# A searched instruction order with longer latencies, one block's K and V loads on the GpSimd queue, and early memsets on VectorE

## The chip, the cores and the metric

The kernel runs on one core of a Trainium2 chip. A core has five engines with instruction streams of their own: TensorE (PE, matrix products), VectorE (DVE), ScalarE (ACT), GpSimd (POOL) and SyncE (SP, which here only issues transfers). The metric is the device time of one execution in microseconds (us); the median of several executions is compared.

## The reference

An attention in which every query sees only six chunks of 32 keys, followed by a two-layer network with an ELU. Cut to what matters:

```python
# q, k, v: (4 batches, 8 heads, 768 positions, 64); w_in (512, 2048); w_out (2048, 512)
k_min, k_max = min and max of k over each chunk of 32 keys          # 24 chunks
ub = sum_d(maximum(q * k_min, q * k_max))                            # upper bound per query and chunk
ub = where(causal by chunk, ub, -1e9)
top_chunks = the 6 chunks with the largest ub, per query
scores = q @ k.T / sqrt(64);  masked to the chosen chunks and to keys not after the query
attn = exp(scores - max) / sum
x = attn @ v, heads side by side                                     # 3072 tokens x 512
h = x @ w_in
g = where(h > 0, h, exp(min(h, 0)) - 1)                              # ELU
out = g @ w_out
```

## The kernel before

The kernel cuts the 3072 tokens into nine blocks: three of 256 queries for the first batch, two of 384 for each of the others. Heads are worked on in four pairs. Each block goes through the same stages, and each stage is a set of small operations that are recorded first, each with an engine, an assumed duration, an assumed latency and what it reads and writes:

```python
def prep_k(j, i):   # pair j, block i: K turned on PE, chunk minima and maxima on DVE, copy to lhs
    turn_in(psk, k_ld, w // P)                                        # PE transposes (float32), L480
    op("DVE", ..., lambda: reduce(kmx..., AOT.max), ...)              # L500
    op("DVE", ..., lambda: reduce(ksts[bp][:, 0, j, cs], AOT.min), ...)
    # copy to lhs: ACT directly for blocks 0 and 1 (L507), else ACT (L512) and a transfer (L515)
def prep_q(j, i):   # Q turned on PE, QTf on ACT (L530), rhs on ACT (L534) or POOL (L538), relu on DVE (L541)
def select(i):      # bounds of all chunks (PE, L559), then on DVE: transposes (L570), MAX8 (L577),
                    # compare (L581), and the mask written into rhs: by DVE transposes (L587) for
                    # blocks 0 to 2, by a transpose and eight transfers (L593, L597) for later ones
def attend(j, i, at):  # scores (PE, L621), exp (ACT, L637), causal triangle (DVE, L648),
                       # weighing of V (PE into o_bank, L670), division (DVE, L679, L681),
                       # turned to xt by PE (L689) or by a transposing transfer (L694)
def mlp(i, at):     # per 128 hidden units: 4 matmuls (L709), exp (ACT, L713), minus 1 (POOL, L715),
                    # min and max into gT (DVE, L717); then 16 matmuls per 128 tokens with w_out (L728)
```

A scheduler inside the kernel then places all operations in time with these assumed durations, taking on each engine the ready operation with the smallest priority number. `SHIFTS` adds a number to the priority for each stage, engine and block; the table was found by search over that model. The resulting order, not the times, becomes the program:

```python
            if done is not None:
                done.end = clock + 750                # a transfer is seen 750 ns after its last byte
...
            else:
                o.end = t + o.occ + o.lat
...
    for o in plan.ops:
        o.prio = o.prio0 + (SHIFTS[o.key[0][0], o.eng][o.key[0][1]] if o.key[0] else 0.0)
    plan.run()
    pe = 0.0
    with tc.manual_schedule():
        for o in plan.order:
            if o.eng == "PE":
                if o.start < FILL_END:
                    for _ in range(int((o.start - pe - 100) / FILL_NS) if pe else int((o.start - FILL_FROM) / 95)):
                        nc.tensor.matmul(o_bank[:, 400:512], lhsT=junk, rhs=junk[:, 0:112], start=True, stop=True)
                pe = o.start + o.occ
            o.fn()
```

The matmuls on `junk` (L836) are fillers: they compute nothing that is used and keep TensorE busy where the model sees a gap in the first 70 us.

At the start, constants and padding are written, mostly by GpSimd, and the first loads are issued from three queues. `SW_LOADS` names those of the GpSimd queue, `SW_ORDER` their order, `ACT_LOADS` those of which one half goes to ScalarE's queue. A gate, a copy of one element of the first K tile, keeps the GpSimd queue from starting before that tile is there:

```python
SW_LOADS = ("v0", "q1", "v1", "k2", "q2", "v2")
ACT_LOADS = ("k0", "q0", "k1")
SW_ORDER = ("v0", "q1", "v1", "wi0", "wi1", "wi2", "wi3", "k2", "q2", "v2", "wo0", "wo1", "wo2", "wo3")
...
    pool_op(150, lambda: nc.gpsimd.memset(junk, 0.0), [r_junk])
    for x in range(2):
        pool_op(650, lambda x=x: nc.gpsimd.memset(ksts[x], 0.0), ...)
    for s in range(NPAIR):
        init_vext(s)
    for h in range(2):
        for x in range(2):
            pool_op(360, lambda h=h, x=x: nc.gpsimd.memset(selb[x][h], 0.0), [r_selb[x][h]])
        pool_op(650, lambda h=h: nc.gpsimd.memset(rhs[0][64:96, h, :, 0:QSEL], 0.0), r_m[0][h])
    ...
        gate_ops.append(op("POOL", 120, 60, lambda: nc.gpsimd.tensor_copy(out=spot[:, 0:1], in_=gx.get()[0:1, 0, 0, 0:1]), ...))
```

Of the kernel before, what the change touches and what calls it, by code (L numbers as in the profile page):

```python
# [32 lines left out]
NPAIR = H // 2  # L33
# [17 lines left out]
PSM_PREP = (0, )  # L51
PSM_S = (0, )
MASK_DVE = (0,1,2)
SW_LOADS = ("v0", "q1", "v1", "k2", "q2", "v2")
ACT_LOADS = ("k0", "q0", "k1")
SW_ORDER = ("v0", "q1", "v1", "wi0", "wi1", "wi2", "wi3", "k2", "q2", "v2", "wo0", "wo1", "wo2", "wo3")
QC_ACT = (0, 1)
VC_ACT = ()
SW_GATE = ("k", 0)
# [4 lines left out]
CAPS = dict(psT=1, psS=2, psO=1, psM=4, kld=2, qld=2, vld=1, QTf=6, Qrl=6, kb=3, kmx=3, ubT=2, thr=2,  # L64
            msk=2, pt=9, rcp=2, on=3, xt=12, gT=6, e=4, osb=2)
RING = 64
FILL_NS = 500
FILL_FROM = 1500
FILL_END = 70e3
SHIFTS = {  # L70
    ('cast', 'POOL'): (20.57252, 6.8612, 30.20405, 34.41781, 25.32335, 14.40461, 26.6349, 11.90162, 25.68724),
    ('gate', 'POOL'): (13.59135, 0.0, 0.0, 0.0, 0.0, 0.0, 0.0, 0.0, 0.0),
    ('init', 'POOL'): (0.0, 2.28733, 0.0, 0.0, 0.0, 0.0, 0.0, 0.0, 0.0),
    ('init', 'SP'): (0.0, 0.0, -9.16794, 0.0, 0.0, 0.0, 0.0, 0.0, 0.0),
    ('kld', 'ACT'): (8.44149, -3.35541, 0.0, 0.0, 0.0, 0.0, 0.0, 0.0, 0.0),
    ('kld', 'SP'): (2.64524, 1.41433, 0.0, 19.17193, 19.24991, 15.09263, 15.30211, 16.29283, 21.31107),
    ('kld', 'POOL'): (0.0, 0.0, 0.38774, 0.0, 0.0, 0.0, 0.0, 0.0, 0.0),
    ('mlp_in', 'ACT'): (-0.05814, -2.04884, 12.26157, -1.88135, -2.65088, -4.49011, 9.3327, 8.76113, -19.73093),
    ('mlp_in', 'DVE'): (-1.73242, 3.97867, -1.47336, 9.41966, -10.49042, -8.87396, -12.71275, -12.8411, -15.53763),
    ('mlp_in', 'PE'): (4.09513, -2.56825, 21.51914, 0.57236, -12.4212, 2.60542, -2.43752, -8.17452, 3.48831),  # L80
    ('mlp_in', 'POOL'): (-2.43649, 11.70673, 2.23367, -14.23721, -5.69178, 14.90153, -11.32679, 8.9361, -11.19179),
    ('mlp_out', 'ACT'): (-12.88274, 0.81443, 16.77095, 16.67571, -11.88345, 9.70583, 0.95732, -8.4172, -1.17404),
    ('mlp_out', 'PE'): (13.70296, 13.79101, 25.0585, 31.67234, 12.47262, 15.64879, 21.01371, 0.27209, 18.2925),
    ('mlp_out', 'SP'): (-3.30971, -11.51233, -15.89764, -18.24659, -18.60542, -17.81261, -26.35693, -42.75655, -13.10907),
    ('prep_k', 'ACT'): (25.42091, 28.44317, 23.77021, 23.42552, 13.97171, 21.34953, 15.42692, 18.62561, 8.78796),
    ('prep_k', 'DVE'): (-0.54594, 19.16199, -1.31495, -4.02643, 4.07559, 21.34444, 2.30963, 13.60589, 3.98678),
    ('prep_k', 'PE'): (-11.58195, 3.17776, 12.63442, -8.97337, 3.48395, 2.91992, -14.39538, 4.89175, 2.89372),
    ('prep_k', 'SP'): (0.0, 0.0, -5.13913, -2.5227, -2.19514, 2.12301, -17.34079, 2.83345, -3.2583),
    ('prep_q', 'ACT'): (-5.44132, 13.02836, -8.90449, 17.58325, 14.42173, 12.5627, 34.41294, 25.56545, -14.46432),
    ('prep_q', 'DVE'): (34.05268, 22.68609, 13.28254, 24.29798, 22.86233, 18.30023, 26.52607, 17.39426, -1.03575),  # L90
    ('prep_q', 'PE'): (1.55827, 3.21992, -10.06088, -5.14194, -2.06832, 11.30076, 4.84068, 13.28142, -17.29924),
    ('prep_q', 'POOL'): (0.0, 0.0, 5.34856, 19.77789, 11.98652, -3.89053, 10.37057, 11.76628, -23.71212),
    ('qld', 'ACT'): (3.03879, 0.0, 0.0, 0.0, 0.0, 0.0, 0.0, 0.0, 0.0),
    ('qld', 'SP'): (-1.86639, 0.0, 0.0, 4.4756, 10.84559, 7.56364, -2.78613, 8.55013, 3.96718),
    ('qld', 'POOL'): (0.0, -13.20166, -16.00657, 0.0, 0.0, 0.0, 0.0, 0.0, 0.0),
    ('score', 'ACT'): (10.38182, 13.98097, 9.11548, 19.0005, 2.98314, 27.9414, -1.05566, 1.31311, 14.18917),
    ('score', 'DVE'): (-19.79772, 4.15071, 2.99001, -22.45535, -14.99666, -19.5343, -10.56439, -19.58759, -3.51749),
    ('score', 'PE'): (-4.26638, 7.52896, -6.42214, -0.75335, 6.37057, 12.51955, 6.09242, -2.75776, -4.26028),
    ('select', 'DVE'): (0.47921, -15.73633, 7.03029, -0.12414, -12.38193, 6.31401, -10.30796, 14.19953, -5.33831),
    ('select', 'PE'): (-24.6966, -18.87682, -19.68284, -16.23997, -30.84817, 2.75471, -0.87585, -4.04933, -12.62166),  # L100
    ('select', 'SP'): (0.0, 0.0, 0.0, -13.44596, -16.7602, -5.46409, -14.4042, 14.89348, -7.20168),
    ('vld', 'POOL'): (8.78219, 3.38089, -2.61859, 0.0, 0.0, 0.0, 0.0, 0.0, 0.0),
    ('vld', 'SP'): (0.0, 0.0, 0.0, 33.2739, 30.57728, 28.35083, 33.49035, 19.69352, 14.95572),
    ('w_in', 'POOL'): (-4.9889, 0.0, 0.0, 0.0, 0.0, 0.0, 0.0, 0.0, 0.0),
    ('w_out', 'POOL'): (-8.71011, 0.0, 0.0, 0.0, 0.0, 0.0, 0.0, 0.0, 0.0),
    ('weigh', 'DVE'): (11.1506, -8.59523, 21.73165, 3.04344, -9.17916, -0.955, 14.23334, -3.50298, 13.22401),
    ('weigh', 'PE'): (-14.42242, 4.04006, -5.56916, -12.49286, -15.03128, -12.17144, 11.16201, -20.81204, -2.27982),
    ('weigh', 'SP'): (0.0, -24.05575, -20.27905, -10.4246, -14.45262, -3.75467, -21.17209, -15.72941, 0.0),
}


# [38 lines left out]
class Plan:  # L150
# [37 lines left out]
    def run(self):  # L188
# [41 lines left out]
        while True:  # L230
# [35 lines left out]
                    dirty.add(e)  # L266
                    room = True
            if done is not None:
                done.end = clock + 750
                lanes[done.eng][done.lane] = done.end  # L270
                dirty.update(("SP", "ACT", "POOL"))
                leave(done, done.end)
                enter(done, done.end, True)
                continue
# [15 lines left out]
            if isinstance(o.lat, tuple):  # L290
                rings[o.eng].append([t + o.occ + o.lat[2], o.lat[0], o.lat[1], o])
                if o.eng != "POOL" and over(o.eng) > 1e-6:
                    full_rings[o.eng], free[o.eng] = free[o.eng], 1e18
                e = lane_of[o.eng]
                o.lane = turn[e]
                lanes[e][o.lane], turn[e] = 1e18, (o.lane + 1) % 8
                dirty.update(("SP", "ACT", "POOL"))
            else:
                o.end = t + o.occ + o.lat
                leave(o, o.end)  # L300
                enter(o, o.end, True)
        assert len(self.order) == len(self.ops)
# [4 lines left out]
def kernel(  # L307
# [120 lines left out]
    def load(dst, x, i, cls, at):  # L428
# [5 lines left out]
        for n in range(nt):  # L434
            at(n / nt)
            e = "POOL" if cls[0] + str(i) in SW_LOADS else "ACT" if cls[0] + str(i) in ACT_LOADS and n == 1 else "SP"

            def go(n=n, q=dict(SP=nc.sync, ACT=nc.scalar, POOL=nc.gpsimd)[e]):
                q.dma_start(out=xb.get()[:, n, :, :], in_=x[b, :, lo + P * n:lo + P * (n + 1)].rearrange("h p d -> p h d"))  # L439

            o = op(e, 890 if e == "POOL" else 600, (770, 159, 1000) if e == "POOL" else dma(64, 256), go,
                   writes=[r], hold=[xb], seq=[*(chain if e == "SP" else ()), *newest.get(cls, ())])
            newest[cls] = [o]
            if e == "SP":
                chain[:] = [o]
            if e == "POOL":
                sw.setdefault(cls[0] + str(i), []).append(o)
        for j in range(NPAIR):
            dst[j, i] = (xb, (r, ), slice(2 * j, 2 * j + 2))

# [303 lines left out]
    def casts(i):  # L754
        at = span(i - 1, 0.5 + SP_F[0], 0.5 + SP_F[1])
        plan.tag = ("cast", i)
        for j in range(NPAIR):
            at(j / NPAIR)
            cast_v(j, i)

    for s in range(NPAIR):
        init_lhs(s, "DVE")
    pool_op(150, lambda: nc.gpsimd.memset(junk, 0.0), [r_junk])
    for x in range(2):
        pool_op(650, lambda x=x: nc.gpsimd.memset(ksts[x], 0.0), [r for j in range(NPAIR) for r in r_kst[x][j]])
    for s in range(NPAIR):
        init_vext(s)
    for h in range(2):
        for x in range(2):
            pool_op(360, lambda h=h, x=x: nc.gpsimd.memset(selb[x][h], 0.0), [r_selb[x][h]])  # L770
        pool_op(650, lambda h=h: nc.gpsimd.memset(rhs[0][64:96, h, :, 0:QSEL], 0.0), r_m[0][h])
    pool_op(300, lambda: nc.gpsimd.tensor_copy(out=ident_b, in_=ident_f), [r_ident_b], [r_ident_f])
    pool_op(900, make_tri, [r_tri])
    gate_ops = []
# [13 lines left out]
    front(0)  # L788
    casts(0)
    plan.tag = ("init", 1)  # L790
    span(-0.5, 0.0, 0.1)
    for s in range(NPAIR, NSET):
        init_vext(s)
    load_kq(1)
# [36 lines left out]
    with tc.manual_schedule():  # L831
        for o in plan.order:
            if o.eng == "PE":
                if o.start < FILL_END:
                    for _ in range(int((o.start - pe - 100) / FILL_NS) if pe else int((o.start - FILL_FROM) / 95)):
                        nc.tensor.matmul(o_bank[:, 400:512], lhsT=junk, rhs=junk[:, 0:112], start=True, stop=True)  # L836
                pe = o.start + o.occ
            o.fn()
# [29 lines left out]
```

## Time and profile before

| | before |
|---|---|
| device time, median of 3 | 306.47 us (304.36 to 306.54) |
| span of the profiled execution | 302.4 us |
| busy PE / DVE / ACT / POOL | 279.0 / 204.9 / 201.3 / 138.9 us |
| mean granted TensorE clock | 0.96 of full |
| bytes moved by DMA | 36.23 MB, mean 120 GB/s |

How to read it: busy time is the time in which an engine has an instruction in flight. Matmuls overlap each other, so the busy time of PE is not the time that its work needs; that is read from how far apart the starts of matmuls lie when nothing holds them. The granted clock is the share of full speed at which TensorE was allowed to run. "Us to landing" of a transfer counts from its issue to the signal that the data is there.

### The profile page before, as it was taken

Reading aid. Unit: us, or ns where it says so; the run is one execution under the profiler, and the core shown is the slowest. Engines: PE = TensorE matmul, PEld = TensorE weight load, DVE = VectorE, ACT = ScalarE, POOL = GpSimd, SP = SyncE. Lnnn points to the kernel's source line nnn. Section 1 sums busy time; section 2 is a strip of 40 time slices with the busy share of each in tenths; the row PEclk is TensorE's granted clock in tenths of the full one; section 3 lists DMA queues with packets and bytes.
Section 4 is the critical chain, followed back from the end, with each engine's and each line's share of the span. In section 5 each row is a group of like instructions: output and inputs, shape, how many; then the busy total and the mean of one; then the engine's idle time right before and its main releaser. Section 6 shows DMA issues by size and latency. Waiting matters only on the chain.

```text
span 302.4 us, 7251 instructions
## 1 busy us (share of the span) xinstructions
PE 279.0 (92%) x2521; PEld 177.4 (59%) x2521; DVE 204.9 (68%) x658; ACT 201.3 (67%) x458; POOL 138.9 (46%) x285
## 2 busy tenths in 40 slices
PE   7466878999999899999999989999999999999994
PEld 7235645677857645666665546666556666554541
DVE  4567488799666979768579955874866646680420
ACT  1764767579829725997797259886398896671521
POOL 8796674024817624571069322581535100570420
PEclk9955797999999999999999999999999999999999
DMA  8769996149292565658239853924111012100101
GB/s 194 204 130 196 292 220 115 41 125 244 48 222 74 133 149 135 162 153 204 81 80 219 191 166 84 233 57 128 47 44 43 3 48 63 30 21 37 67 37 70
DMA packets 88805, 36.23 MB, mean 120 GB/s; under 512 B 76224, under 2 KB 84928, under 8 KB 88768
## 3 DMA queue, kind: packets, MB, share of 16 engines
q1 hardware_dynamic: 80464, 27.64, 36.3%
q0 software_dynamic: 5184, 7.34, 12.0%
q10 hardware_dynamic: 3120, 0.79, 1.2%
q8 instruction: 20, 0.33, 0.4%
q14 instruction: 17, 0.14, 0.1%
HBM read 27.26 MB, written 6.29 MB: 111 GB/s over the span
## 4 chain that ended last, share of the span: by engine, by line
PE 64%; DVE 14%; DMA 7%; POOL 6%; SPq 3%; ACT 2%; issue 2%; POOLq 0%; DVEq 0%; ACTq 0%
PE psM L728 22%; PE psM L709 18%; PE psS L621 10%; PE o_bank L670 6%; PE psT L480 5%; DVE gT L717 3%; DMA rhs<-msk 3%; DVE rhs L587 2%; POOL e L715 2%; SPq L439 2%; DMA vld<-in_v_dram 2%; DVE kmx L500 2%; PE psT L559 1%; DMA qld<-in_q_dram 1%; DVE pt L648 1%
## 5 line engine op out<-in xcount | busy, mean ns | idle before, releaser
L715 POOL TENSOR_SCALAR e<-e 128x384 f32<-128x384 f32 (+1 forms) x144 | 68.2, 479 | 106.4 <-ACT e L713 67.5
L709 PE MATMUL psM<-xt,w_in_sb 128*128 128x384 bf16 (+1 forms) x576 | 102.4, 313 | 1.8 <-DVE gT L717 1.5
L728 PE MATMUL psM<-w_out_sb,gT 128*128 128x512 bf16 x384 | 102.8, 379 | 0.0
L637 ACT ACTIVATE pt<-psS 128x384 bf16<-128x384 f32 (+1 forms) x164 | 83.4, 546 | 10.5 <-PE psS L621 9.0
L717 DVE SCALAR_TENSOR_TENSOR gT<-psM,e 128x384 bf16<-128x384 f32 (+1 forms) x144 | 70.8, 508 | 27.9 <-POOL e L715 24.6
L713 ACT ACTIVATE e<-psM 128x384 f32<-128x384 f32 (+1 forms) x144 | 66.0, 465 | 22.0 <-PE psM L709 20.5
L709 PEld LDWEIGHTS <-w_in_sb 128*128 128x128 bf16 x576 | 56.1, 100 | 29.5 <-issue 2.8
L621 PE MATMUL psS<-rhs,lhs 96*128 96x256 bf16 (+2 forms) x304 | 65.1, 287 | 4.3 <-DMA rhs<-msk 1.6
L728 PEld LDWEIGHTS <-gT 128*128 128x128 bf16 x384 | 36.3, 98 | 31.9 <-issue 2.1
L538 POOL TENSOR_SCALAR rhs<-QTf 64x384 bf16<-64x384 f32 (+1 forms) x56 | 29.7, 531 | 29.5 <-ACT QTf L530 21.9
L621 PEld LDWEIGHTS <-lhs 96*128 96x128 bf16 x312 | 28.2, 100 | 22.1 <-issue 4.3
L670 PEld LDWEIGHTS <-pt 128*128 128x128 bf16 x672 | 28.9, 99 | 11.2 <-DVE pt L648 2.1
L670 PE MATMUL o_bank<-vext,pt 128*128 128x65 bf16 x672 | 32.7, 195 | 2.0 <-DVE pt L648 1.3
L732 ACT ACTIVATE osb<-psM 128x512 f32<-128x512 f32 x24 | 14.5, 604 | 28.0 <-PE psM L728 27.9
L530 ACT ACTIVATE QTf<-psT 128x384 f32<-128x384 f32 (+1 forms) x32 | 15.3, 478 | 10.6 <-PE psT L480 10.2
L471 POOL TENSOR_SCALAR vext<-vld 128x384 bf16<-128x384 f32 (+1 forms) x36 | 17.4, 504 | 10.2 <-DMA vld<-in_v_dram 9.9
L648 DVE TENSOR_TENSOR pt<-pt,tri 128x512 bf16<-128x512 bf16 x36 | 17.1, 476 | 7.3 <-ACT pt L637 6.7
L512 ACT ACTIVATE kb<-psT 128x384 bf16<-128x384 f32 (+1 forms) x28 | 13.5, 483 | 11.8 <-DVE kst L500 8.0
L500 DVE TENSOR_REDUCE kmx<-psT 128x12 f32<-128x384 f32 (+1 forms) x32 | 16.5, 516 | 6.6 <-PE psT L480 6.3
L480 PE MATMUL psT<-ident_f,qld 128*128 128x128 f32 x88 | 16.5, 291 | 4.3 <-DMA qld<-in_q_dram 3.3
L541 DVE TENSOR_SCALAR Qrl<-QTf 128x192 f32<-128x192 f32 (+3 forms) x36 | 12.2, 349 | 10.3 <-ACT QTf L530 10.1
L681 DVE TENSOR_TENSOR on<-o_bank,rcp 128x384 bf16<-128x384 f32 (+1 forms) x36 | 18.3, 508 | 0.8 <-DVE rcp L679 0.3
(69 smaller groups left out, 241.7 us busy)
## 6 DMA issues: line engine op xcount, KB each, us to landing
out_dram<-osb SPq DMA_DIRECT2D x24, 256.0 KB, 2.2
kld<-in_k_dram SPq DMA_DIRECT2D x20, 256.0 KB, 3.7
qld<-in_q_dram SPq DMA_DIRECT2D x19, 256.0 KB, 4.2
vld<-in_v_dram SPq DMA_DIRECT2D x18, 256.0 KB, 3.7
lhs<-kb SPq DMA_DIRECT2D x48, 48.0 KB, 1.9
w_in_sb<-in_moe_w_in_dram POOLq DMA_DIRECT2D x4, 512.0 KB, 10.4
w_out_sb<-in_moe_w_out_dram POOLq DMA_DIRECT2D x4, 512.0 KB, 10.4
vld<-in_v_dram POOLq DMA_DIRECT2D x6, 256.0 KB, 4.3
```

Source lines behind the costliest of these rows:

```text
L480: nc.tensor.transpose(ps.get()[:, P * n:P * (n + 1)], xb.get()[:, n, hs, :].rearrange("p h d -> p (h d)"), ident_f)
L500: nc.vector.tensor_reduce(out=out, in_=psk.get()[:, 0:w].rearrange("p (c w) -> p c w", w=CHUNK), axis=AX.X, op=o)
L538: pool_op(110 + pool_ns(w), lambda h=h: nc.gpsimd.tensor_scalar(out=rhs[RH[i]][0:64, h, j, 0:w], in0=qtf.get()[64 * h:64 * h + 64, 0:w], s ...
L621: nc.tensor.matmul(sps.get()[:, o + pc:o + pc + n], lhsT=lhs[s][0:96, hd, P * kb:P * (kb + 1)], rhs=rhs[y][0:96, hd, j, c0 - lo:c0 - lo + ...
L637: op("ACT", act_ns(wtot), 140, lambda pt=pt, sps=sps, hd=hd, wtot=wtot: nc.scalar.activation(out=pt.get()[:, hd, 0:wtot], in_=sps.get()[:, ...
L648: nc.vector.tensor_tensor(out=view, in0=view, in1=tri01[:, :].rearrange("p (a b w) -> p a b w", a=1, b=1) .to_broadcast([P, 2, 2, P]), op= ...
L670: nc.tensor.matmul(o3.get()[:, hd, qi, :], lhsT=pt.get()[:, hd, P * qt + off:P * qt + off + P], rhs=vexts[s][:, kb, hd, :], start=(kb == 0 ...
L709: op("PE", 1 + w / 2.4, 200, lambda fc=fc, kk=kk, h_ps=h_ps: nc.tensor.matmul(h_ps.get()[:, 0:w], lhsT=w_in_sb[:, kk, P * fc:P * (fc + 1)] ...
L713: op("ACT", act_ns(w), 200, lambda e=e, h_ps=h_ps: nc.scalar.activation(out=e.get()[:, 0:w], in_=h_ps.get()[:, 0:w], func=AF.Exp), reads=[ ...
L715: op("POOL", pool_ns(w), 72, lambda e=e: nc.gpsimd.tensor_scalar(out=e.get()[:, 0:w], in0=e.get()[:, 0:w], scalar1=-1.0, scalar2=1.0, op0= ...
L717: g_ops.append(op("DVE", dve_ns(w), 130, lambda e=e, h_ps=h_ps, fc=fc: nc.vector.scalar_tensor_tensor(out=gT[fc // 4].get()[:, fc % 4, 0:w ...
L728: op("PE", 216, 200, lambda tt=tt, fc=fc, o_ps=o_ps: nc.tensor.matmul(o_ps.get(), lhsT=gT[fc // 4].get()[:, fc % 4, P * tt:P * (tt + 1)], ...
```

## The change

The scheduler's model is made more cautious: a transfer counts as seen 1500 ns after its last byte instead of 750, and every operation's result is seen 80 ns later. With that model the priorities were searched anew, so the whole `SHIFTS` table is replaced and nearly every instruction moves on its engine. The second block's K, which went over the SyncE and ScalarE queues, goes to the front of the GpSimd queue. The early memsets of `junk`, `ksts`, `selb` and of the mask rows of `rhs[0]` go from GpSimd to VectorE. Within one load, the pieces need no longer be issued one after the other in their order (`newest`). The number of fillers ahead of the first real matmul is worked out with 90 ns each instead of 95. Arithmetic, tiles, buffers and the amount of work stay as they are.

```diff
-SW_LOADS = ("v0", "q1", "v1", "k2", "q2", "v2")
-ACT_LOADS = ("k0", "q0", "k1")
-SW_ORDER = ("v0", "q1", "v1", "wi0", "wi1", "wi2", "wi3", "k2", "q2", "v2", "wo0", "wo1", "wo2", "wo3")
+SW_LOADS = ("k1","q1","v0","v1","k2","q2","v2")
+ACT_LOADS = ("k0", "q0")
+SW_ORDER = ("k1","v0","q1","v1","wi0","wi1","wi2","wi3","k2","q2","v2","wo0","wo1","wo2","wo3")
...
+DMA_END = 1500
+MARGIN = 80
...
 SHIFTS = {
-    ('cast', 'POOL'): (20.57252, 6.8612, 30.20405, ...),
+    ('cast', 'POOL'): (23.69201, -1.09103, 8.72813, ...),
...  (every row has new numbers; a row for ('init', 'DVE') is new)
-                done.end = clock + 750
+                done.end = clock + DMA_END
...
-                o.end = t + o.occ + o.lat
+                o.end = t + o.occ + o.lat + MARGIN
...
-            newest[cls] = [o]
+            last = [o]
...
+        newest[cls] = last
...
+    op("DVE", 70, 60, lambda: nc.vector.memset(junk, 0.0), writes=[r_junk])
...
-    pool_op(150, lambda: nc.gpsimd.memset(junk, 0.0), [r_junk])
+    for h in range(2):
+        op("DVE", 390, 60, lambda h=h: nc.vector.memset(rhs[0][64:96, h, :, 0:QSEL], 0.0), writes=r_m[0][h])
     for x in range(2):
-        pool_op(650, lambda x=x: nc.gpsimd.memset(ksts[x], 0.0), ...)
+        op("DVE", 160, 60, lambda x=x: nc.vector.memset(ksts[x], 0.0), ...)
+        for h in range(2):
+            op("DVE", 170, 60, lambda h=h, x=x: nc.vector.memset(selb[x][h], 0.0), writes=[r_selb[x][h]])
...
-    for h in range(2):
-        for x in range(2):
-            pool_op(360, lambda h=h, x=x: nc.gpsimd.memset(selb[x][h], 0.0), [r_selb[x][h]])
-        pool_op(650, lambda h=h: nc.gpsimd.memset(rhs[0][64:96, h, :, 0:QSEL], 0.0), r_m[0][h])
...
-                    for _ in range(int((o.start - pe - 100) / FILL_NS) if pe else int((o.start - FILL_FROM) / 95)):
+                    for _ in range(int((o.start - pe - 100) / FILL_NS) if pe else int((o.start - FILL_FROM) / 90)):
```

The words "first V" in the change's description show in `SW_LOADS` and `SW_ORDER`: the first block's V stays on the GpSimd queue and now comes second there, behind K of the second block.

## The prediction

> **What bounds the kernel now.** I read the page's first part and its slices first, then the stretches between changes of the granted clock, then the chain and the timeline of the first 50 us. The page says PE is the fullest engine, and where it is not full:
>
> ```profile
> PE 279.0 (92%) x2521; PEld 177.4 (59%) x2521; DVE 204.9 (68%) x658; ACT 201.3 (67%) x458; POOL 138.9 (46%) x285
> ...
> PE   7466878999999899999999989999999999999994
> ...
> PEclk9955797999999999999999999999999999999999
> ```
>
> After the seventh slice (53 us) PE is at 9 nearly throughout, and the low clock lies in slices 3 to 6. Busy time overstates PE, so I counted what its work needs: every matmul at the distance of starts that the trace shows when nothing holds it. That is 216 ns for 512 columns (48 of L728 take 10.36 us in the chain), 162 for 384 (52 of L709 take 8.45), 109 for 256, 56 for 128, 30 for the 65 of L670, 111 for a float32 transpose, and about 9 us for all bounds (0.7 to 1.5 a block). Fillers count nothing. The sum is 254.3 us. The *lag* is the time of a matmul's start less the work ahead of it in the program. From the timeline: lag 16.8 at the first scores (18.6 us), 24.3 at the first L709 (30.1), 30.7 at the second block's first scores (45.4), 34.0 at 52 us, 39.8 at 145, 42.6 at 183, 44.2 at the last matmul (298.3). The output after it takes the last 4.1 us. So 34 of 48 us that are not work are lost in the first 52 us, some 9 us between there and 185, and 1.6 after. The stretches show the same:
>
> ```profile
> 13.60:34.10 20.50, 14.47 (x118) 9.81 (x119) 11.74 (x48) 13.03 (x34) 15.32 (x24) 0.50 0.96 197
> 34.10:47.70 13.60, 10.14 (x101) 6.76 (x100) 11.21 (x45) 9.59 (x26) 11.00 (x26) 1.00 1.21 227
> 47.70:51.20 3.50, 3.29 (x18) 2.10 (x16) 3.25 (x9) 2.46 (x6) 0.95 (x3) 0.52 0.62 114
> ...
> 185.00:298.50 113.50, 113.31 (x952) 66.94 (x949) 65.73 (x185) 75.87 (x163) 43.41 (x84) 1.00 0.22 63
> ```
>
> Columns: stretch, length, busy of PE, weight loads, DVE, ACT, POOL, clock, DMA share, GB/s. For 20.5 us and again for 3.5 us PE ran at half clock. In the last stretch nothing is left to gain but 0.2 us. What holds the start is in the timeline and the chain:
>
> ```profile
> 7.79 0.76 DVE L500 TENSOR_REDUCE kmx<-psM 128x8 f32<-128x256 f32 x2 [2.90 <-PE psM L480]
> ...
> 8.65 0.18 POOL L782 COPY spot<-kld 1x1 f32<-1x1 f32 x1
> 8.77 2.01 POOL L439 DMA_DIRECT2D vld<-in_v_dram  x2
> ...
> 10.77 1.76 POOL L439 DMA_DIRECT2D qld<-in_q_dram  x2
> ...
> 15.94 0.47 PE L480 MATMUL psT<-ident_f,qld 128*128 128x128 f32 x1 [0.86 <-DMA qld<-in_q_dram]
> ...
> 16.35 0.47 PE L559 MATMUL psM<-QTf,kst 64*32 64x64 f32 x16
> ```
> ```profile
> 42.15 0.71 DVE ubT L570 x2
> 42.86 1.14 DVE thr L577 x16
> 44.00 0.85 DVE selb L581 x2
> 44.88 0.44 DVE rhs L587
> ```
>
> GpSimd opens its gate only at 8.65 us, after its memsets, though the first K half had landed at 0.81 + 3.6 = 4.4 us. So the second block's Q lands at 15.9, and the first bounds, ready at about 14, wait behind its transposes in PE's order. Later the second block's bounds come at 40.9, and eight DVE masks after them pace the scores until 48.6.
>
> [...] fillers start 93 ns apart, 49 ns from 6.8 us on, and the boundaries at 13.6, 34.1, 47.7 and 51.2 lie multiples of 3.4 apart. [...] with DMA 83% busy the first 13.6 us moved 198 GB/s. [...] Here L728 lasts 379 ns on average but starts every 216, which is why I use the lag.
>
> **The change, part by part.** Positions are from the two programs' instruction orders; times from rows of the trace before.
>
> 1. *Early memsets.* GpSimd loses junk 0.20, kst 1.39, selb 1.63 + 0.77, rhs 0.74 + 0.73, together 5.5 us of what stood before the gate. The gate could be reached at 3.2, so it waits for K and opens at about 4.7. VectorE gains about 2 us (a DVE copy of 768 bf16 elements took 0.64 us; I count some 2,100 four-byte elements and nine starts). It stood idle for 2.90 us before its first reduction, so this is hidden.
> 2. *Fillers.* They need junk only, which DVE has by about 1.05 instead of 2.23. They become 79 instead of 60. If the clock rises at 6.8 again: 62 at 93 ns, 17 at 49, ending at 7.65 against 7.36, a loss of 0.3. [...] I count nothing.
> 3. *Loads.* Behind the gate come K1 (0.95 each, as the second K issues took), V0, Q1: V0 is issued at 6.6 instead of 8.77, Q1 at 8.6 instead of 10.77. Bandwidth limits it: ten tiles of 256 KB and four of 96 KB are 3.0 MB, at 198 / 0.83 = 239 GB/s 12.6 us, so Q1 lands not before 14.5, 1.4 sooner. K1 lands at about 10 to 11, is first used near 13, and so costs nothing.
> 4. *First bounds.* In the new order they come before Q1's transposes and behind one pair of K1. They start at about 14.0 instead of 16.35. From there to the first scores DVE does two transposes 0.54, memsets 0.12, MAX8 0.43, compares 0.36, one mask 0.26 and 0.8 of start: 16.5 instead of 18.55. Gain 2.0.
> 5. *First L709.* ACT now does four QTf (0.38), four pairs of rhs copies (0.84), eight exps (0.5) and one lhs copy (0.38) from about 16.5 on: 9.3, to 25.8. The last pair's triangle, weighing, division, turn and copy add 3: 29 instead of 30.1. But 6.4 us of work lie before it instead of 5.8. Gain in lag 1.7, which contains step 4.
> 6. *Second block's selection.* Its bounds move from 43 matmuls of the first block's L709 ahead of them to 16: 29 + 16 x 0.213 is 32.4, say 33 instead of 40.9. The first mask follows after 4.0 as before, 2.6 for reductions and gT placed in between, and 0.4: 40.0. Before its scores lie 12.8 us of work instead of 14.7. Lag 27.2 instead of 30.7: gain 3.5, which contains 4 and 5.
> 7. *Masks and half clock from 45 to 51.* Lag grew there by 3.3. With L709 left to put between (21 matmuls among the new scores, 8 before) I give back 1.0 of it. Sum so far 4.5.
> 8. *The rest, 52 us on.* Work between a block's bounds and its first scores, in PE's order, before and after: block 2 4.3 and 5.8; 3 6.5 and 7.8; 4 8.7 and 8.8; 5 11.0 and 7.6; 6 9.1 and 16.0; 7 19.4 and 7.2; 8 28 and 10. The short ones grow, the long ones shrink but stay above 7. Lag grew by 10.2 there before; I take 1.5 off. The end is the same: 48 of L728 after the last L709, then 4.1.
>
> Sum 6.0: 306.5 - 6.0 = 300.5.
>
> **Rivals.**
> *The start is bound by bandwidth, not by order.* For: DMA share is 1.21 and 227 GB/s from 34 to 48, and w_in took 7.7 to 13.1 us to land. Against: L709 never waited for w_in on PE. If w_in lands after 29, or K2 late, steps 5 to 7 shrink to the first 2 us: 304.
> *A new wait takes over in the middle.* The search shortens the way of blocks 5, 7 and 8, where masks go by eight transfers at 0.6 issue and 1.8 landing each, after 3 to 4 of DVE: up to 10 us against 7.2. For: PE waited 1.6 us in all for such masks, 1.3 of it at once. Against: scores of later pairs need only later masks. This would cost 2 to 4 us: 303 to 305.
> *PE stays warm.* If the fuller start keeps the clock up from 20 us on, half of some 6 us of cold work comes back, and MLP matmuls move sooner too: 295 to 297. Against: in 13.6 to 34.1 the gaps come from ACT and DVE, which the change does not make shorter.
> *A cautious model spreads things too far* and gives nothing: 306. Every landing in the trace (1.8 to 13 us) is longer than an optimistic model supposes, which speaks against it.
>
> **Range and chances.** The start gives 2 to 7, the middle -3 to +4, and three runs before differ by 2.2. Together: 295 to 306, centre 300.5. The 2% line is 300.3, almost at the centre; so faster by over 2% 0.48, within 2% 0.48, slower by over 2% 0.04.
>
> **What would show it.** Right: the first vld issue on GpSimd before 7 us; L559 first at about 14; the second block's first L621 at 38 to 42; lag about 29 to 30 at 52 us (the loss between there and the end near 9). Step 1 is wrong if DVE's first reduction starts after 8.5. Step 6 is wrong if DVE idles before MAX8 or PE waits for w_in. The prediction is wrong above 306 if PE waits for rhs<-msk or vld grow to several us after 100 us, and below 295 if the clock is full before 30 us.

## The result, and the profile after

The changed kernel takes 297.75 us (median of 4, 296.48 to 298.15), the kernel before on the same chip 305.54 (median of 4, 304.36 to 306.54). The ratio is 0.9739, with a 95% interval of 0.9685 to 0.9794. A ratio leaves out executions that were unusually slow for their kernel and a median does not, so two experiments can rank differently by the two. The profiled execution went from 302.4 to 295.9 us. That of the kernel before took 304.14 us in all, 1.4 us less than its median, so the two traces differ by 6.5 us and the medians by 7.8.

The lines of the page after that answer to those shown of before (busy time and instructions of each engine, then the slices of the span):

```profile
PE 277.3 (94%) x2544; PEld 179.4 (61%) x2544; DVE 204.8 (69%) x667; ACT 196.4 (66%) x458; POOL 137.0 (46%) x278
...
PE   8576879999999998999999999999999999999993
...
PEclk9865798999999999999999999999999999999999
```

PE is no busier than before; the span around it is shorter. There are 23 more matmuls, all fillers, and the first slices are only a little fuller (8576879 against 7466878). So the gain is not to be read from these lines. The windows of the changed kernel (stretch, length, busy of PE, weight loads, DVE, ACT, POOL, then clock, DMA share, GB/s) say as little:

```profile
13.60:34.10 20.50, 15.82 (x156) 10.43 (x155) 14.25 (x55) 14.48 (x40) 16.11 (x26) 0.60 0.98 202
34.10:47.70 13.60, 11.12 (x93) 8.68 (x91) 12.57 (x50) 9.62 (x25) 9.54 (x22) 0.87 1.21 198
47.70:51.20 3.50, 3.50 (x40) 2.72 (x39) 3.29 (x11) 3.50 (x10) 1.32 (x3) 1.00 0.61 126
```

The clock in the first stretch is 0.60 instead of 0.50, and the second stretch of half clock has moved from 47.8 to 43.7 us. What either is worth is taken up below. The timeline of the changed kernel shows the steps of the start (start, length, engine, line, operation; in brackets the idle time before and what ended it):

```profile
4.63 0.23 POOL L795 COPY spot<-kld 1x1 f32<-1x1 f32 x1 [1.23 <-DMA kld<-in_k_dram]
4.80 2.01 POOL L442 DMA_DIRECT2D kld<-in_k_dram  x2
6.80 1.76 POOL L442 DMA_DIRECT2D vld<-in_v_dram  x2
...
7.81 0.76 DVE L504 TENSOR_REDUCE kmx<-psM 128x8 f32<-128x256 f32 x2 [0.61 <-PE psM L484]
...
8.55 1.76 POOL L442 DMA_DIRECT2D qld<-in_q_dram  x2
...
13.41 0.73 PE L563 MATMUL psM<-QTf,kst 64*32 64x64 f32 x16 [1.04 <-ACT QTf L534]
...
28.64 3.62 PE L713 MATMUL psM<-xt,w_in_sb 128*128 128x256 bf16 x16
...
48.33 0.38 PE L732 MATMUL psM<-w_out_sb,gT 128*128 128x512 bf16 x1
```

Lines are numbered a little higher in the changed kernel: bounds are L563 (was L559), scores L625 (L621), weighing L674 (L670), the two products of the network L713 and L732 (L709 and L728). GpSimd now waits for K at its gate (1.23 us idle) and not for its own memsets. The V load is issued 2.0 us sooner, Q of the second block 2.2 us. DVE's first reduction is where it was, with 0.61 us of idle time ahead of it where there had been 2.90: the memsets took the place of idling. The first product with w_out, which closes the start in what follows, stood here in the kernel before:

```profile
51.53 0.60 PE L728 MATMUL psM<-w_out_sb,gT 128*128 128x512 bf16 x2
```

### Where the time came from

The lag of the prediction, start of a matmul less the work ahead of it, splits the gain. At the first product with w_out (L728, now L732), and at the last matmul:

| us | before | after | gain |
|---|---|---|---|
| lag at the first w_out product | 33.7 | 29.9 | 3.8 |
| growth from there to the last matmul | 10.4 | 7.2 | 3.2 |
| last matmul to the end | 4.3 | 4.8 | -0.5 |

So in these two traces about half comes from the first 50 us and half from the 240 us after them. The second half is almost invisible in the views of idle time. PE's waits from 52 us on (in total, times, longest), the larger ones of the kernel before:

```profile
PE psS L621 <- DMA rhs<-msk: 1.6, 2, 1.3
PE o_bank L670 <- DVE pt L648: 0.8, 1, 0.8
PE o_bank L670 <- DVE pt L655: 0.4, 2, 0.3
```

and of the changed kernel:

```profile
PE psS L625 <- DMA rhs<-msk: 1.5, 2, 1.0
PE o_bank L674 <- DVE on L685: 0.5, 1, 0.5
PE psT L484 <- DMA kld<-in_k_dram: 0.3, 1, 0.3
```

With the small ones, 3.5 us before and 2.8 after: 0.7 of the 3.2 us. The rest lies in gaps which the overlapping ends of matmuls cover (a w_out product lasts 379 ns in both traces and starts 216 ns after the one before it). To find them I let every matmul whose lag is above all earlier ones add the difference to its line:

| growth of the lag after the first w_out product | before | after |
|---|---|---|
| pushed up by scores | 3.8 | 2.6 |
| by weighing | 2.8 | 1.4 |
| by products with w_in | 1.7 | 1.1 |
| by bounds, transposes and products with w_out | 2.1 | 2.0 |
| of all this, at places of 0.3 us and more | 5.1 (9 places) | 3.6 (6 places) |

Weighing waits for exponentials and triangles, scores for masks. That the new order leaves these more time, at many places by a few tenths each, is argued from this table and not shown by a run.

One trace of each kernel is little. In this and four other traces with the changed order (those below that have all records of matmuls), scores push the lag up by 0.9 to 2.6, weighing by 1.1 to 1.4 and the products with w_in by 1.1 to 1.8. So what weighing lost is well known, what scores lost is not, and for w_in nothing can be told. The growth as a whole is clear of such spread: 5.5 to 7.7 us in the seven traces that have the changed order throughout, against 10.4, 12.3 and 13.4 in the three with the old order. (Where some 27 records of w_out products are missing, their work is counted all the same.) The 12.3 and 13.4 belong to old orders with a start 1.4 and 1.1 us sooner, a lead that was gone by the last matmul. Start and rest may thus not simply add up; with one trace each this can't be told from the difference between executions.

### The profile page after: what moved, and what is told of

Same layout as the page of the kernel before. It is cut to its first block, busy times and chain, and to the rows that moved or that the text cites. A ratio compares the mean times of both kernels' runs of the same rounds, so it can differ in the third digit from the quotient of the medians.

```text
span 295.9 us, 7293 instructions
## 1 busy us (share of the span) xinstructions
PE 277.3 (94%) x2544; PEld 179.4 (61%) x2544; DVE 204.8 (69%) x667; ACT 196.4 (66%) x458; POOL 137.0 (46%) x278
## 4 chain that ended last, share of the span: by engine, by line
PE 73%; DVE 13%; ACT 6%; DMA 4%; issue 2%; POOL 1%; SPq 0%; POOLq 0%; DVEq 0%; ACTq 0%
PE psM L713 23%; PE psM L732 23%; PE psS L625 10%; PE o_bank L674 6%; PE psT L484 5%; DVE gT L721 3%; PE psT L563 2%; DMA rhs<-msk 2%; PE o_bank L849 2%; ACT rhs L538 2%; DVE rhs L591 2%; DVE kmx L504 2%; ACT lhs L511 1%; DMA kld<-in_k_dram 1%; DVE thr L581 1%
## 5 line engine op out<-in xcount | busy, mean ns | idle before, releaser
L719 POOL TENSOR_SCALAR e<-e 128x384 f32<-128x384 f32 (+1 forms) x144 | 69.8, 489 | 120.6 <-ACT e L717 60.0
L713 PE MATMUL psM<-xt,w_in_sb 128*128 128x384 bf16 (+1 forms) x576 | 109.0, 313 | 1.6 <-DVE gT L721 1.4
L732 PE MATMUL psM<-w_out_sb,gT 128*128 128x512 bf16 x384 | 99.1, 379 | 0.0
L641 ACT ACTIVATE pt<-psS 128x384 bf16<-128x384 f32 (+1 forms) x164 | 87.7, 568 | 13.2 <-PE psS L625 12.7
L717 ACT ACTIVATE e<-psM 128x384 f32<-128x384 f32 (+1 forms) x144 | 68.8, 486 | 21.9 <-PE psM L713 18.4
L713 PEld LDWEIGHTS <-w_in_sb 128*128 128x128 bf16 x576 | 55.4, 99 | 28.1 <-issue 2.4
L625 PE MATMUL psS<-rhs,lhs 96*128 96x384 bf16 (+2 forms) x304 | 66.3, 286 | 2.5 <-DMA rhs<-msk 1.5
L732 PEld LDWEIGHTS <-gT 128*128 128x128 bf16 x384 | 36.0, 98 | 31.5 <-issue 1.2
L625 PEld LDWEIGHTS <-lhs 96*128 96x128 bf16 x312 | 29.4, 100 | 19.4 <-issue 2.3
L736 ACT ACTIVATE osb<-psM 128x512 f32<-128x512 f32 x24 | 14.4, 600 | 30.5 <-PE psM L732 30.3
L674 PEld LDWEIGHTS <-pt 128*128 128x128 bf16 x672 | 27.8, 99 | 9.8 <-issue 1.7
L674 PE MATMUL o_bank<-vext,pt 128*128 128x65 bf16 x672 | 30.9, 195 | 0.8 <-DVE on L685 0.5
L484 PE MATMUL psT<-ident_f,kld 128*128 128x128 f32 x88 | 16.0, 285 | 1.3 <-ACT QTf L534 0.6
```

What stands on the lines that cost most here:

```text
L484: nc.tensor.transpose(ps.get()[:, P * n:P * (n + 1)], xb.get()[:, n, hs, :].rearrange("p h d -> p (h d)"), ident_f)
L625: nc.tensor.matmul(sps.get()[:, o + pc:o + pc + n], lhsT=lhs[s][0:96, hd, P * kb:P * (kb + 1)], rhs=rhs[y][0:96, hd, j, c0 - lo:c0 - lo + ...
L641: op("ACT", act_ns(wtot), 140, lambda pt=pt, sps=sps, hd=hd, wtot=wtot: nc.scalar.activation(out=pt.get()[:, hd, 0:wtot], in_=sps.get()[:, ...
L674: nc.tensor.matmul(o3.get()[:, hd, qi, :], lhsT=pt.get()[:, hd, P * qt + off:P * qt + off + P], rhs=vexts[s][:, kb, hd, :], start=(kb == 0 ...
L713: op("PE", 1 + w / 2.4, 200, lambda fc=fc, kk=kk, h_ps=h_ps: nc.tensor.matmul(h_ps.get()[:, 0:w], lhsT=w_in_sb[:, kk, P * fc:P * (fc + 1)] ...
L717: op("ACT", act_ns(w), 200, lambda e=e, h_ps=h_ps: nc.scalar.activation(out=e.get()[:, 0:w], in_=h_ps.get()[:, 0:w], func=AF.Exp), reads=[ ...
```

## The experiments

The theory to test, mine: the gain comes from the order, in its two halves, start and rest; memsets and the queue of K only make the new start possible. Rivals: the placements alone bring it (GpSimd's gate), the first bounds alone bring it, or the fuller start brings it by its clock. The ratios below are to the kernel before, run beside each on the same chip (its median 305.5 to 306.3 us), with their 95% intervals. Where an experiment rearranges the program, it does so after the kernel's scheduler is done and keeps all other instructions and fillers in their places, unless it says otherwise.

### The changed kernel again

No edit. It gives the spread from one execution to another, beside the experiments that share its chip.

> The changed kernel itself once more, on the same chip as the next three, as their measure. Every theory: 0.970 to 0.980 of the kernel before, about 297.7 us.

Median 295.57 us (295.16 to 299.83), ratio 0.9664 (0.9624 to 0.9703), lower than the expected 0.970 to 0.980. The profiled execution spans 293.4, 2.5 us less than the first. The two traces part in the first 50 us, in which the second is 2.2 us ahead; the growth after it is 6.9 against 7.2:

```profile
46.10 0.38 PE L732 MATMUL psM<-w_out_sb,gT 128*128 128x512 bf16 x1
```

0.6 us of this is there at the first reduction (7.24 for 7.81). Most of the rest goes with the clock:

```profile
34.10:47.70 13.60, 10.99 (x100) 8.35 (x99) 13.26 (x51) 10.96 (x29) 9.51 (x24) 1.00 1.20 197
```

Here no second stretch of half clock came (1.00 instead of 0.87). What that stretch costs can be read: over the last 40 matmuls ahead of the first w_out product, fillers left out, the lag grew by 2.3 us in the first trace and by 0.9 here. The other traces with the changed start fall into the same two groups, 2.2 to 2.4 in the four that have such a stretch and 0.9 in the three that don't. So 3.4 us of half clock cost 1.4 us at this place. The kernel before has such a stretch too, at 47.8, so it isn't what the first pair of traces gained by. Against this kernel's own spread, differences of 1 to 2 us in one trace mean nothing.

### Memsets back on GpSimd

```diff
-    op("DVE", 70, 60, lambda: nc.vector.memset(junk, 0.0), writes=[r_junk])
+    op("DVE", 70, 60, lambda: nc.gpsimd.memset(junk, 0.0), writes=[r_junk])
     (likewise rhs, kst and selb; in the program all nine stand behind GpSimd's second own constant)
```

> The changed kernel with its order on every engine kept, only the nine early memsets back on GpSimd ahead of the gate. My theory (the order makes the gain, and the memset move is what lets K1 go behind the gate): the gate opens at 8.7 us instead of 4.6, K1 lands at 14 to 15 although PE wants it at 11.9, and the first bounds stand behind it: the bounds slip from 13.4 to about 15.5 to 16, the time grows by 2 to 3 us, to about 300. Rival (the memsets don't matter because GpSimd is not the bound): within 0.5 us of the changed kernel.

Median 300.20 us, ratio 0.9806 (0.9763 to 0.9850), 4.6 us above the changed kernel on the same chip, with intervals apart. Its timeline:

```profile
8.80 0.18 POOL L795 COPY spot<-kld 1x1 f32<-1x1 f32 x1
8.92 2.01 POOL L442 DMA_DIRECT2D kld<-in_k_dram  x2
...
14.86 0.48 PE L484 MATMUL psT<-ident_f,kld 128*128 128x128 f32 x1 [1.63 <-DMA kld<-in_k_dram]
...
16.27 0.47 PE L563 MATMUL psM<-QTf,kst 64*32 64x64 f32 x16 [0.75 <-DVE Qrl L545]
```

The gate opens at 8.80, K of the second block leaves at 8.92, and PE stands 1.63 us for it, ahead of the first bounds in its queue. The time is as expected (about 300), and its distance from the changed kernel beside it larger than the 2 to 3 us. The new order and the new queue for K need the early gate.

### The second block's K back on SyncE and ScalarE

```diff
-            def go(n=n, q=dict(SP=nc.sync, ACT=nc.scalar, POOL=nc.gpsimd)[e]):
+            def go(n=n, q=(nc.sync, nc.scalar)[n] if cls == "kld" and i == 1 else dict(SP=nc.sync, ACT=nc.scalar, POOL=nc.gpsimd)[e]):
     (and these two loads stand right behind the first block's Q in those queues)
```

> The changed kernel with its order kept, only K1 issued again by SyncE and ScalarE at the start, as before. My theory: V0 and Q1 are issued 2 us sooner, but nothing in the new order waits for them on PE, so the time stays within 0.7 us of the changed kernel. Rival (the move to the GpSimd queue keeps K1's bytes out of the way of K0 and Q0, and that is a part of the gain): first reduction on DVE later than 7.8 us, Q0's transposes later than 10.1, and 1 to 2 us more.

Median 297.09 us, ratio 0.9718 (0.9671 to 0.9765). It lies 1.5 us above the changed kernel beside it, and the intervals overlap: no difference can be told. In the trace the first reduction starts at 7.45 and the first bounds at 13.05 (12.84 in the changed kernel's second trace). K or Q of the first block is not held up by the K loads behind them. So with the gate early, the new queue for K brings nothing that these runs can measure.

### Both back: the new order alone

Both edits above together.

> The changed kernel's order on every engine with the placement of before: memsets on GpSimd and K1 on SyncE and ScalarE. This is the order alone. My theory: V0 and Q1 are issued at 8.8 and 10.8 and land at 13 and 16, Q1 just where the new order wants it (16.3); K1 is early; so the order alone gives nearly the whole gain: within 1 us of the changed kernel, 297.5 to 299. Rival (placement makes the gain of the start, 3.6 us of the 7): 301 to 302.

Median 298.74 us, ratio 0.9764 (0.9722 to 0.9806): the order alone keeps 7.5 of the 10.7 us that the changed kernel gained on this chip, and the placements add about 3. That is in the expected 297.5 to 299, but it isn't within 1 us of the changed kernel beside it; of the changed kernel's first measurement (297.75) it is. What is lost shows at the very start of the traced execution (299.93 us):

```profile
9.45 0.76 DVE L504 TENSOR_REDUCE kmx<-psM 128x8 f32<-128x256 f32 x2 [4.41 <-PE psM L484]
...
15.09 0.68 PE L563 MATMUL psM<-QTf,kst 64*32 64x64 f32 x16 [1.08 <-ACT QTf L534]
```

The 79 fillers now start at 2.59, when GpSimd has written `junk`, and end at 9.18; the first transposes of K stand behind them, and the first reduction is 2.2 us later than with the early memset (7.24). Part of that is the moment at which the clock rose, read from the distance of the fillers: with the memsets back alone, the 79 fillers also start at 2.59 but end at 7.91, the last 19 of them 49 ns apart where the last 34 here are 67 ns apart on average, and the first reduction stands at 8.18. So between 0.9 and 2.2 us of the start are lost with the late `junk` here, and the number of fillers fits the early `junk` only.

### The old order with the new placements

```diff
-    pool_op(150, lambda: nc.gpsimd.memset(junk, 0.0), [r_junk])
+    pool_op(150, lambda: nc.vector.memset(junk, 0.0), [r_junk])
     (likewise rhs ahead of DVE's first copies, kst and selb behind the first; K of block 1 by
      nc.gpsimd right behind the gate; all else in the order of the kernel before)
```

> The kernel before with its order on every engine kept, and only the placement changed: the nine memsets on VectorE, K1 behind the gate of the GpSimd queue. My theory (placement alone helps only as far as Q1 lands sooner; the order then wastes it): Q1 lands near 14 instead of 15.9, the first bounds come at about 14.5 instead of 16.4, and of that 1 to 2 us arrive at the end: 304 to 305.5 for 306.3. Rival (placement makes the start's gain): 3.5 us, 302.5 to 303.

Median 303.92 us over 20 runs, ratio 0.9968 (0.9934 to 1.0003): no gain that can be told from none, and at most 0.7% by the interval. And yet it did what it should at the start: the first bounds came at 14.35 and the first scores at 16.48, instead of 16.35 and 18.55. Of these two microseconds 1.1 were left at the first w_out product:

```profile
50.42 0.63 PE L728 MATMUL psM<-w_out_sb,gT 128*128 128x512 bf16 x1
```

After it the lag grew by 13.4 (10.4 before), so none was left at the end; this trace is of the slowest of the 20 executions (306.23 us). The times rule out the rival that the placements bring the gain by themselves.

### The first bounds ahead of the second Q, in the old order

```diff
     order of the kernel before; then
+    move(ops of prep_q(1) from its first PE op, behind the last bound of select(0))   # on PE only
```

> The kernel before with one move in PE's order: the first bounds ahead of the first transposes of Q1, which land at 15.9. My theory (step 4 of the prediction): bounds at 14.0 instead of 16.35 and the first scores 2 us sooner; by 52 us 1 to 2 us of it are left, since the second block's bounds still stand behind 43 matmuls of L709: 304.3 to 305.3. Rival (the chain through V0, its casts and ACT holds the start, not the bounds): no change, 306.

Median 304.53 us, ratio 0.9897 (0.9826 to 0.9968).

```profile
13.93 0.46 PE L559 MATMUL psM<-QTf,kst 64*32 64x64 f32 x9 [1.50 <-ACT QTf L530]
...
17.19 0.84 PE L621 MATMUL psS<-rhs,lhs 96*128 96x256 bf16 x4
```

Bounds 2.4 us sooner, scores 1.4 sooner, and the lag at the first w_out product 32.3 instead of 33.7. Behind it the lag grew by 12.3. One swap on one engine is worth about 1 us of the 8 by the medians (1 to 5 by the interval of the ratio); the rest of the start needs the other moves too.

### New start, old rest

```diff
+    order = [all up to the first w_out product, as in the changed kernel] + [what is left, as in the kernel before]
```

> The changed kernel's placement and order up to the first matmul of L728 (52 us), then the order of before. My theory (the gains of start and rest add up): lag at 52 us as in the changed kernel, 28 to 30.5, then growth as before, about 10: 301.5 to 303. Rival (a good start carries the rest: its transfers and buffers come sooner, whatever the order): growth 7, 298 to 299.

Median 303.33 us, ratio 0.9914 (0.9879 to 0.9949). That is just above what the theory said. The start is the changed one (lag 30.3 at the first w_out product), and the growth after it is 12.7, that of the old order. At the seam operations of the two orders don't fit, which costs on its own:

```profile
PE psM L713 <- DMA xt<-on: 2.7, 3, 1.1
```

Neither kernel has this wait in such size. If a seam only costs, which is argued and not shown, 0.9% (2.6 us, 1.6 to 3.7 by the interval) is a lower bound for the start.

### Old start, new rest

```diff
+    order = [all up to the first w_out product, as in the kernel before] + [what is left, as in the changed kernel]
```

> The kernel before up to the first matmul of L728 (52 us), then the changed kernel's order. My theory (they add up): lag 34 at 52 us as before, then growth of about 7 instead of 10.2: 302.5 to 303.5. Rival (the rest gains only through the start): growth 10, 306.

Median 301.28 us, ratio 0.9852 (0.9812 to 0.9893). That is better than the theory said. The lag at the first w_out product is 35.5, worse than before (33.7), and the growth after it only 5.6. So the new rest brings 1.5% (4.5 us, 3.3 to 5.7 by the interval) with the old start and placements, and the rival that the rest gains only through the start is out. With the run above, 7.1 us of the 8 to 10 are found, 2.6 by the start and 4.5 by the rest; as both have a seam, this is a rough split.

### The start sooner still

```diff
-            op("DVE", 660, 60, lambda: nc.vector.tensor_copy(out=lhs[s][64:96], in_=view), reads=[r_econst], writes=r_lhs[s])
+            op("DVE", 660, 60, lambda: nc.sync.dma_start(out=lhs[s][64:96], in_=view), reads=[r_econst], writes=r_lhs[s])
+    fills[first] = 42      # instead of 79
     (the four later transfers of the same kind stand behind a load of the fourth block)
```

DVE's four copies (2.93 us) become transfers, and the fillers end when K is there.

> The changed kernel with its order, except that the four copies of the constant rows into lhs[0..3] (2.9 us of DVE before its first reduction) go as SyncE transfers, those of lhs[4..7] go after the fourth block's first K loads, and 42 fillers stand before the first matmul instead of 79. My theory (the first 7.8 us are held by fillers and these copies, not by K, which has landed at 4.4 to 4.9): first transposes at 5.0 to 5.3 instead of 7.4, first bounds 1.5 to 2 us sooner, and 1 to 2 us less in the end: 0.963 to 0.969 of before, 294.5 to 296.5. Rival (the transfers take bandwidth from Q0, K1 and Q1, and what is won at the start is lost waiting for them): PE waits for a load, no gain, 0.97 or more.

Median 295.07 us, ratio 0.9675 (0.9624 to 0.9727), not to be told from the changed kernel. Its start is ahead of the changed kernel's second trace, which has the reduction at 7.24, the first bounds at 12.84 and the first scores at 16.25:

```profile
5.39 0.76 DVE L504 TENSOR_REDUCE kmx<-psM 128x8 f32<-128x256 f32 x2 [1.30 <-PE psM L484]
...
11.76 0.47 PE L563 MATMUL psM<-QTf,kst 64*32 64x64 f32 x16 [0.84 <-DVE Qrl L545]
...
14.43 0.85 PE L625 MATMUL psS<-rhs,lhs 96*128 96x256 bf16 x4
```

Where the second block's bounds begin it is still ahead (29.51 against 31.78), but the first w_out product comes at 45.88 against 46.10. Of the 2.3 us 1.7 are given back within the second block's bounds:

```profile
29.90 0.76 POOL L463 DMA_DIRECT2D w_out_sb<-in_moe_w_out_dram  x1 [1.41 <-DMA w_in_sb<-in_moe_w_in_dram]
30.68 1.50 POOL L719 TENSOR_SCALAR e<-e 128x256 f32<-128x256 f32 x4
31.13 1.51 DVE L721 SCALAR_TENSOR_TENSOR gT<-psM,e 128x256 bf16<-128x256 f32 x4 [3.25 <-POOL e L719]
31.61 0.40 PE L563 MATMUL psM<-QTf,kst 64*32 64x256 f32 x1 [1.49 <-DVE gT L721]
```

By the trace PE stands 1.49 us for a psM buffer that DVE frees, DVE for GpSimd's minus 1, and this stands in GpSimd's queue behind a load of w_out, whose issue waited for w_in to land. In the changed kernel's second trace the same issue is at 28.92 and the minus 1 at 29.70, 1 us sooner than here: the sooner start of PE meets a GpSimd that is no sooner. This is near to the rival (time lost waiting for transfers), only that GpSimd waits and not PE. It is read from one trace; no run takes that waiting away.

### More fillers

```diff
-                    for _ in range(int((o.start - pe - 100) / FILL_NS) ...
+                    for _ in range(int((o.start - pe - 100) / 160) ...     # behind the first matmul; FILL_NS is 500
```

> The changed kernel with 69 more fillers in the gaps that the model sees after the first transposes (one for each 160 ns instead of 500). Theory of the half clock (the low clock from 13 to 33 us costs part of the start): granted clock 13.6 to 34.1 above 0.75 instead of 0.60, and 1 to 2 us less, 295 to 296.5. My theory (the start hangs on ACT and DVE, and fillers in PE's queue stand before real matmuls): the clock rises, but the time stays within 1 us of the changed kernel or grows by up to 1.5.

Median 297.00 us, ratio 0.9722 (0.9678 to 0.9767): no gain over the changed kernel (297.75 in its first measurement, 295.57 on this chip). Yet the clock did rise, from 0.60 to 0.75 in the stretch of 20 us and to full between 34 and 52:

```profile
13.60:34.10 20.50, 15.82 (x183) 12.09 (x191) 13.69 (x54) 14.66 (x40) 14.86 (x24) 0.75 0.98 201
```

In the trace two things nearly cancel. The second block's bounds come at 33.34, 1.1 us later than in the first trace (32.28) and 1.6 later than in the second (31.78), though the clock was higher on the way. From there to the first w_out product it takes 14.3 us, as in the second trace (14.3) and not as in the first (16.1), since no second stretch of half clock came. Fillers and clock can't be parted in this run, but they can in the others. In three traces (the first one, both back, new start with old rest) the clock was full for 3.4 us between 19.8 and 25.1; in three (the second one, K back, the seam that follows) it was half all that time. From the first bounds to the second block's all six take 18.9 to 19.0 us. ACT is nearly always busy there and GpSimd always, here in the first and the second trace (columns as above):

```profile
19.80:25.10 5.30, 3.29 (x35) 2.01 (x33) 3.89 (x15) 5.19 (x16) 5.29 (x9) 0.82 1.21 198
19.80:25.10 5.30, 3.86 (x30) 2.39 (x28) 4.28 (x14) 5.00 (x14) 5.30 (x9) 0.50 1.23 198
```

So half clock doesn't bind there, and the rival of a warmer PE falls for this part; right ahead of the first w_out product it binds, and costs the 1.4 us above. That one of these two binds in the first part is argued from these lines and the gaps in front of PE; no run took their work away.

### A seam at the third block's middle

```diff
+    order = [all up to the first w_out product of the third block, as in the changed kernel] + [what is left, as before]
```

> The changed kernel's order up to the first matmul of L728 of the third block (99 us in the changed kernel), then the order of before. With the seam at 49 us 303.3 were measured, with no seam 297.8 and 295.6. If what the new order saves after the start lies in the first half of the rest (lag from 18 to 65 us of work grew by 3.9 before and 2.2 after): 300 to 301.5. If it lies in the second half (65 to 145: 4.6 and 3.7), or if any seam costs: 302 to 303.5.

Median 302.07 us, ratio 0.9886 (0.9857 to 0.9915). The lag at the first w_out product of the first block is 28.1, and the growth after it 13.0. About 4 us of it come right at the seam, between 65 and 75 us of work. This was to show how the rest's gain is spread, and it doesn't: the cost of the seam can't be told from that of the old order behind it.

Not tried: old priorities in the cautious model, and new ones in the old model. With either mix the kernel's scheduler finds no complete order. So whether the longer latencies or merely another search made the order better stays open.

## Why the prediction was right, and where it was off

The time, 297.75, lies 2.75 below the predicted 300.5 and inside the range. The mechanism was right too: moves in the order make most of the gain, the steps of the start came within about 1 us of their times, and what was too small is the term for the rest. In the two traces errors of both signs partly cancel: the start brought 3.8 instead of 4.5, the rest 3.2 instead of 1.5, the end lost 0.5, in all 6.5 for 6.0. The centre is nearer to the traces than to the medians (7.8).

1. *Early memsets*: right. The gate opened at 4.63 (predicted 4.7), the first reduction stood at 7.81 (7.79 before). The memsets' groups (count, busy, mean ns), before:

```profile
L770 POOL MEMSET selb<- 128x384 bf16 x4 | 2.4, 629 | 0.1
L765 POOL MEMSET kst<- 128x256 f32 x2 | 1.4, 721 | 0.0
```

and after:

```profile
L779 DVE MEMSET selb<- 128x192 uint32 x4 | 0.8, 218 | 0.0
L777 DVE MEMSET kst<- 128x256 f32 x2 | 0.5, 272 | 0.1
```

With `rhs` and `junk` 5.5 us on GpSimd became 2.2 on DVE. The row for selb carries half as many elements, of four bytes: 192 of these took 218 ns and the 256 of kst 272, 1.1 ns each in both.

2. *Fillers*: right to count nothing. They ended at 7.54 here, and between 6.60 and 7.75 in five other executions with the same 79 from 1.1 us on; by these ends the clock didn't rise at the same moment in each. The prediction's case, a rise at 6.8, gave 7.65. The second stretch of half clock began at 47.8 in the kernel before and at 43.7 after; what sets it off, these runs don't show.

3. *Loads*: V at 6.80 (predicted 6.6), Q at 8.55 (8.6), no wait for the second block's K on PE. Right, and it only holds with step 1, as the memsets put back show. From issue to landing the loads took longer, V 4.9 and 5.1 us instead of 3.7 and 3.9 and Q 4.8 and 6.0 instead of 3.8 and 4.3, so Q's second half was there at 15.4, only 0.5 sooner than before, where the prediction had 1.4. That bandwidth limits these loads was an estimate, which no run here shows; its 239 GB/s is no limit, as 288 GB/s were moved between 3.4 and 6.8 us in the kernel before.

4. *First bounds*: 13.41 for 14.0; first scores 16.81 for 16.5. Right in time. That it is worth 2 us of the total by itself is not: put alone into the old order it gave 1.4 in lag at the first w_out product, and about 1 in the median. (The lag of 16.8 at the first scores of before is a slip: 20 transposes and one set of bounds, 2.9 us, lie ahead of 18.55, which leaves 15.6. No later step uses it.)

5. *First product with w_in*: 28.64 for 29. Right.

6. *Second block's selection*: bounds at 32.28 for 33, first scores at 38.94 for 40.0, lag there 26.0 for 27.2. Right.

7. *Masks and half clock from 45 on*: the lag at the first w_out product is 29.9, where I had 29.5 for 52 us. The start brought 3.8 us instead of 4.5 in this trace, in which a stretch of half clock came at 43.7, and 6.0 in the second trace, without it. The step is right within what varies from one execution to the next.

8. *The rest*: the term that was mis-sized. "I take 1.5 off" became 3.2 in the traces and 4.5 (3.3 to 5.7) by the run with the old start. I had looked at how much work PE has between a block's bounds and its first scores, which bears on masks alone. Scores did lose 1.2 us of growth in the first pair (3.8 to 2.6), about what I took, but up to 2.9 in the other traces. What I left out is weighing, which lost 1.4 in that pair and up to 1.7 in the others. It waits for ACT and DVE; that the search had moved these apart too, and not selections alone, is the likely reason, which no run isolates.

The end, predicted to be the same, lost 0.5 us. Of the rivals, bandwidth did not bind PE (it never waited for w_in), but w_in holds GpSimd's queue, and with a start sooner still that took the gain. No new wait came in the middle (1.5 us for masks against 1.6). A warmer PE is worth 1.4 us where the second stretch of half clock stays away, which happened in some executions and not in others; more clock between 19.8 and 25.1 us was worth nothing. The cautious model did not spread things too far.

What stays open: why the rest is better, the latencies in the model or just another search; and how the rest's gain is spread over the blocks, since seams cost as much as they are to show.

## What to carry to other kernels

A load, a memset or a filler was worth here only what the order behind it could use: bounds 2 us sooner through a sooner load gave 0.3% (within the error) in the old order, and another 1 to 2 us gave nothing in the new one, where GpSimd stood waiting for w_in. So re-search the order after moving such pieces, and their fillers with it. Follow a gain at the start to the last matmul before you count it. Measure the small gaps by starts less work ahead, for half of this gain lay where the views of waits showed 0.7 us of 3.2. And take several traces of a kernel before you split a gain between its parts.

## What was unexpected in the hardware

- It matters where half clock falls: 3.4 us of full clock instead of half between 19.8 and 25.1 us changed nothing (18.9 to 19.0 us from the first bounds to the second block's, with and without), while 3.4 us of half clock right ahead of the first w_out product cost 1.4 us.
- The clock rises and falls at different times from execution to execution: the same 79 fillers ended between 6.60 and 7.75 us, and a second stretch of half clock came or stayed away; the two traces of one program differ by 2.2 us of lag at the first w_out product.
- Four memsets of 12 elements on GpSimd took 0.72 us together from 3.45 on in the kernel before, while DVE was copying, and 0.31 at 8.47, while it was reducing; in the changed kernel 0.31 and 0.30, while DVE was writing memsets. Why was not tried.
